# One fused layer, forward and backward: key and query projections in turns, earlier value rows, an earlier output gradient, and x kept in the home of w2

## The chip, the core and the metric

The kernel runs on one core of a Trainium2 chip. The metric is device time in microseconds (us) of one execution; lower is better. PE is the matrix engine, DVE the vector engine, ACT the scalar engine, POOL the general engine, which also issues DMAs, and SP an engine that does nothing but issue DMAs. Each engine works off its own instructions strictly in order; between engines there are only semaphores.

## The reference

One transformer layer on 2048 tokens of width 512, in bf16: an attention sublayer and a feed-forward sublayer, each behind a layer norm and inside a residual sum. The kernel returns the layer's output and the gradients with respect to x, wqkv, wo, w1, b1, w2 and b2, for a given output gradient.

```python
def _A_ref(x, wqkv, wo):                 # 32 heads of 16
    W, dil = 8, 2
    q, k, v = ...                        # x @ wqkv, split by heads
    idx = pos[:, None] - (jnp.arange(W) * dil)[None, :]
    ...                                  # keys and values at idx, masked where idx < 0
    logits = jnp.einsum("bhsd,bhswd->bhsw", q, kg) * scale
    attn = _softmax(logits, axis=-1)
    o = jnp.einsum("bhsw,bhswd->bhsd", attn, vg)
    return (...) @ wo
def _B_ref(x, w1, b1, w2, b2):
    return _gelu(x @ w1 + b1) @ w2 + b2
h  = x + _A_ref(_layernorm(x), A_wqkv, A_wo)
h2 = h + _B_ref(_layernorm(h), B_w1, B_b1, B_w2, B_b2)
# and jax.vjp of this with respect to all operands but B_x
```

So every token attends to eight tokens: itself and those 2, 4, ... 14 places back.

## The kernel before, in words

The 2048 tokens are four chunks of 512 (`NC` = 4, `CH` = 512). There are three stages.

**Stage 1, attention forward** (lines 346 to 516). For each chunk `c` these helpers run:

- `p1_ln` (L352): SP loads the rows of x, DVE forms statistics (L196, L197), POOL the inverse deviation `rstd` (L201), DVE the normalised rows `ln1` (L205); POOL stores them in DRAM (`ln_d`, L181), PE transposes them (L189) and ACT copies the result to `ln1T` (L190). There are three buffers for x of chunks 0 to 2, one for chunk 3, and one buffer for `ln1`.
- `p1_qk` (L374): `p1_proj` (L366) makes four groups of the key (`kt`), then four of the query (`qt`). A group is four matmuls `ps_qkv` (L370) and one ACT copy (L372). Three small columns of the key go on to the next chunk (DVE copy L383).
- `p1_dots` (L398): for each of the four groups DVE multiplies query and shifted keys (`pr`, L259), and PE sums the products into the logits `ps_L` (L263). There are two product buffers.
- `p1_sm1`, `p1_sm2` (L403, L425): softmax, as a chain over engines: ACT `asb`, DVE `m` (L409), ACT `m1h`, DVE `m` (L413), ACT `m2h`, DVE `m` (L417), PE L419, ACT `e` (L422), PE `ps_sum` (L430), DVE reciprocal (L434), PE `ps_r` (L437), ACT `rb` (L439), DVE `attn` (L440).
- `p1_v` (L388): the value projection, PE transposes to token order (`ptm`, L237), ACT copies `tmst` (L240), SP stores rows `v_d` (L242). `p1_tm` (L394) does the same for key and query, `k_d` and `q_d`.
- `p1_o(c, 0)` and `p1_o(c, 1)` (L443): POOL gathers rows of `v_d` into `R` (L251; two buffers), DVE multiplies them with the attention weights (`prb`, L289), PE sums (`ps_band`, L294), ACT copies `ost` (L453), POOL stores `o_d` (four DMAs, L456), PE transposes (`ptu`, L306), ACT copies `oT` (L307).
- `p1_d` (L459): output projection `ps_wo` with x added by an identity matmul (L466, L467), ACT copies `h` (L468), then the second layer norm into `ln2T`.

`p1_round(c)` (L489) mixes these over neighbouring chunks. Inside a round the program calls `p1_ln(c+2)`, `p1_dots(c+1)`, `p1_d(c-1)`, `p1_qk(c+2)`, `p1_sm1(c+1)`, `p1_o(c,0)`, `p1_v(c+1)`, `p1_sm2(c+1)`, `p1_o(c,1)`, `p1_tm(c+1)`. The framework's scheduler settles the final order of each engine's instructions in stages 1 and 2; the order of calls is its priority. It also inserts the waits, among them those of a buffer for its last readers.

**Stage 2, feed-forward, forward and backward** (lines 518 to 754). `p2_h(c)` (L558) makes the hidden layer in four blocks of up to four column tiles: PE `ps_h` (L571), ACT L572 and L573, then a chain of DVE operations and one ACT sigmoid (L576 to L584), which leaves the activation `gt` and its derivative `dt`; SP transposes `gt` by DMA (`tst`, L555), POOL stores it (`gT_d`, L556). `p2_rest(c)` (L590) makes the layer's output with w2 (`ps_f`, L602), then the gradient of the hidden layer: PE `ps_gg` (L615), from the transposed output gradient `goT` and the transposed weights `w2T`, and DVE L617, which multiplies it into `dt`; then the gradient of the layer norm's output, `ps_gl` (L626), with the transposed `w1T`. SP issues the transposing DMAs in this order: `woT`, three parts of `w2T` (L703), four parts of `w1T` (L705), stores of the hidden layer, and then `goT` of chunk 0 (L594).

**Stage 3, attention backward and weight gradients** (from line 760) has an order written out by hand and is not touched.

**Weights.** w1 and w2 (in three parts each, homes `w10`, `w18`, `w112` and `w20`, `w28`, `w212` of the pool `wff`) are loaded by POOL near the start (L485, L487). At the very start SP issues, in this order: the biases b1 and b2 (L149, L151), x of chunk 0, four small stores of zero rows (L347), three parts of wqkv (L358), x of chunks 1 to 3 (L178).

Of the kernel before, what the change touches and what calls it, by code (L numbers as in the profile page):

```python
# [10 lines left out]
P = 128  # L11
BF16 = mybir.dt.bfloat16
# [8 lines left out]
PAD = 16  # L21
# [15 lines left out]
def kernel(  # L37
# [108 lines left out]
    rstd1 = const.tile([P, NT], F32, name="rstd1")  # L146
    rstd2 = const.tile([P, NT], F32, name="rstd2")
    b1b = const.tile([FT, P], BF16, name="b1b")
    SY.dma_start(out=b1b[:], in_=B_b1.rearrange("(f p) -> f p", p=P))  # L149
    b2row = const.tile([1, D], BF16, name="b2row")  # L150
    SY.dma_start(out=b2row[:], in_=B_b2.rearrange("(a n) -> a n", a=1))  # L151
    b1c = const.tile([P, FT], F32, name="b1c")
    gb1p = const.tile([P, FT, NC], F32, name="gb1p")

# [181 lines left out]
                return t_[:, f - a, :]  # L336

    w1 = wparts(wff, "w1", W3, False)
    w2 = wparts(wff, "w2", W3, True)
    late = LP("late")  # L340
    early = LP("early", "right")

    wqkv = early.tile([P, DC, 3 * D], BF16, name="wqkv")
    wo = late.tile([P, DC, D], BF16, name="wo")

    for (d_t, r) in ((v_d[0], 0), (k_d[0], 0), (q_d[NC - 1], CH), (go_d[NC - 1], CH)):
        SY.dma_start(out=d_t[r:r + RPAD, :], in_=zrow[:])  # L347

    st_ = [dict() for _ in range(NC)]
    h_all = []  # L350

    def p1_ln(c):  # L352
        xt = (early if c < NC - 1 else late).tile([P, TPC, D], BF16, name="xt", tag="xt", bufs=NC - 1 if c < NC - 1 else 1)
        load_rows(xt, xf, c)
        if c == 0:
            for i in range(3):
                o = (1, 0, 2)[i] * D
                SY.dma_start(out=wqkv[:, :, o:o + D], in_=A_wqkv[:, o:o + D].rearrange("(a p) j -> p a j", p=P))  # L358
        ln1 = early.tile([P, TPC, D], BF16, name="ln1", tag="ln1", bufs=1)
        layernorm(early, xt, rstd1, c, ln1)  # L360
        store_rows(ln1_d, c, ln1)
        ln1T = early.tile([P, DC, CH], BF16, name="ln1T", tag="ln1T", bufs=2)
        to_fm(ln1, ln1T)
        st_[c].update(xt=xt, ln1T=ln1T)

    def p1_proj(c, sel, dst, off):  # L366
        for g in range(4):
            ps = X("ps_qkv")
            for dc in range(DC):
                T.matmul(ps[:], lhsT=wqkv[:, dc, sel * D + g * P:sel * D + (g + 1) * P],  # L370
                         rhs=st_[c]["ln1T"][:, dc, :], start=(dc == 0), stop=(dc == DC - 1))
            A.copy(out=dst[:, g, off:off + CH], in_=ps[:])  # L372

    def p1_qk(c):  # L374
        qt = early.tile([P, 4, CH], BF16, name="qt", tag="qt", bufs=2)
        kt = early.tile([P, 4, PAD + CH], BF16, name="kt", tag="kt", bufs=2)
        if c == 0:
            V.memset(kt[:, :, 0:PAD], 0.0)
            zz = early.tile([P, 4, PAD], BF16, name="zz", tag="zz")
            V.memset(zz[:], 0.0)  # L380
            G.dma_start(out=vf_d[:, :, 0:PAD], in_=zz[:])
        else:
            V.tensor_copy(out=kt[:, :, 0:PAD], in_=st_[c - 1]["kt"][:, :, CH:CH + PAD])  # L383
        p1_proj(c, 1, kt, PAD)
        p1_proj(c, 0, qt, 0)
        st_[c].update(qt=qt, kt=kt)

    def p1_v(c):  # L388
# [9 lines left out]
    def p1_dots(c):  # L398
        d = st_[c]
        d["L"] = [X("ps_L") for _ in range(2)]  # L400
        dots(late, d["qt"], d["kt"], d["L"], c == 0)
# [73 lines left out]
    p1_ln(0)  # L475
    p1_qk(0)
    p1_dots(0)
    G.dma_start(out=wo[:], in_=A_wo.rearrange("(a p) j -> p a j", p=P))
    p1_ln(1)
    p1_v(0)  # L480
# [2 lines left out]
    p1_sm2(0)  # L483
    for a_, b_, t_ in w1:
        G.dma_start(out=t_[:], in_=B_w1[:, a_ * P:b_ * P].rearrange("(a p) f -> p a f", p=P))  # L485
    for a_, b_, t_ in w2:
        G.dma_start(out=t_[:], in_=B_w2[a_ * P:b_ * P, :].rearrange("(a p) d -> p a d", p=P))  # L487
    p1_tm(0)
    def p1_round(c):  # L489
        if c + 2 < NC:  # L490
            p1_ln(c + 2)
        if c + 1 < NC:
            p1_dots(c + 1)
        if c > 0:
            p1_d(c - 1)
        if c + 2 < NC:
            p1_qk(c + 2)
        if c + 1 < NC:
            p1_sm1(c + 1)
        p1_o(c, 0)  # L500
        if c == NC - 1:
            return
        p1_v(c + 1)
        p1_sm2(c + 1)
        p1_o(c, 1)
        p1_tm(c + 1)
        if c == 0:
            pb = TT("pb1")
            T.transpose(pb[:, 0:FT], b1b[:], ident[0:FT, 0:FT])
            V.tensor_copy(out=b1c[:], in_=pb[:, 0:FT])  # L510
# [79 lines left out]
    def p2_rest(c):  # L590
        d = ps2[c]
        gts, dts = d["g"], d["d"]
        goT = ft("goT")
        SY.dma_start_transpose(out=goT[:], in_=gof[c * CH:(c + 1) * CH, :])  # L594
        gout = ft("gout")
        load_rows(gout, gof, c)
        ln2 = ft("ln2r")
        load_rows(ln2, ln2_d, c)
        for j in range(TPC):
            ps = psT.tile([P, 512], F32, name="ps_f2", tag="t")  # L600
            for f in range(FT):
                T.matmul(ps[:], lhsT=gts[f // 4][:, f % 4, j * P:(j + 1) * P], rhs=wrow(w2, f), start=(f == 0), stop=False)  # L602
            T.matmul(ps[:], lhsT=ones_row[:], rhs=b2row[:], start=False, stop=False)
            T.matmul(ps[:], lhsT=ident[:], rhs=h_all[c][:, j, :], start=False, stop=True)
            h2s = ft("h2s")
            A.copy(out=h2s[:], in_=ps[:])
            A.dma_start(out=h2f[c * CH + j * P:c * CH + (j + 1) * P, :], in_=h2s[:])
            yield
        for bi, (f0, f1) in enumerate(FB):
            for fp in range(f0, f1, 2):  # L610
                for i in range(2):
                    f = fp + i
                    ps = Y("ps_gg")
                    for dc in range(DC):
                        T.matmul(ps[:], lhsT=wcol(w2T, dc, f), rhs=goT[:, dc, :], start=(dc == 0), stop=(dc == DC - 1))  # L615
                    dsl = dts[bi][:, f - f0, :]
                    V.tensor_tensor_reduce(out=dsl, in0=ps[:], in1=dsl, scale=1.0, scalar=0.0,  # L617
                                           op0=ALU.mult, op1=ALU.add, accum_out=gb1p[:, f, c:c + 1])
                yield
            tok_store(dts[bi], f0, f1, ghT_d, c)  # L620
        gh = htile(f"gh{c}")
        gh_all[c] = gh
        for j in range(TPC):
            ps = psT.tile([P, 512], F32, name="ps_gl2", tag="t")
            for f in range(FT):
                T.matmul(ps[:], lhsT=dts[f // 4][:, f % 4, j * P:(j + 1) * P], rhs=wrow(w1T, f),  # L626
                         start=(f == 0), stop=(f == FT - 1))
            t = c * TPC + j
            ln_bwd(ffp["B"], ps[:], ln2[:, j, :], rstd2[:, t:t + 1], gout[:, j, :], gh[:, j, :])
            yield  # L630
# [70 lines left out]
    w1T = wparts(wfb, "w1T", W4, True)  # L701
    for a_, b_, t_ in w2T:
        SY.dma_start_transpose(out=t_[:], in_=B_w2[a_ * P:b_ * P, :])  # L703
    for a_, b_, t_ in w1T:
        SY.dma_start_transpose(out=t_[:], in_=B_w1[:, a_ * P:b_ * P])  # L705
    run(hn)
# [496 lines left out]
```

## Time and profile before

| what | value |
|---|---|
| median of 6 executions | 691.83 us (685.3 to 698.63) |
| the profiled execution | 693.65 us, of which its span is 691.6 us |
| busy in the span | PE 614.7 us (89%), DVE 513.6 (74%), ACT 368.4 (53%), POOL 148.6 (21%) |
| mean granted clock of PE | 0.973 |
| PE busy, 0 to 177 us (stage 1 and the first hidden blocks) | 140.4 us |
| DVE busy, 0 to 177 us | 148.9 us |
| PE and DVE busy, 204 to 260 us (stage 2) | 54.7 and 43.7 us of 56 |

The span runs from the first to the last instruction of the profiled execution; the rest of its time (693.65 - 691.6 = 2.05 us) lies around it. Times in the traces count from the start of the span. A line of a timeline gives the start, the length, the engine, the source line, the operation with output and inputs, how many instructions are merged (x8), and in brackets how long the engine had been idle before and what released it. Busy times of the stretches in the last three rows are sums over a table of stretches of the span.

### The profile page before, as it was taken

What the parts mean: (1) busy time and instruction counts of PE and PEld (TensorE: products, weight loads), DVE (VectorE), ACT (ScalarE), POOL (GpSimd) and SP (SyncE); (2) the same over time, 40 slices, a digit from 0 to 9 for tenths busy, and PEclk for the clock granted to TensorE, in tenths of its full rate; (3) what the DMA queues carried; (4) which work ended last, traced back from release to release, by engine and by line L of the source; (5) the groups of instructions that cost most, each with busy time, mean ns of one, the idle gap of its engine ahead of it and who ended that gap; (6) DMA issues with size and microseconds to landing.
All of it is one profiled execution on the core that took longest, in us unless ns stands there. A gap on an engine that the chain in (4) does not pass through costs nothing. (4 is left out here: it accounts for less than half of the span.)

```text
span 691.6 us, 10209 instructions
## 1 busy us (share of the span) xinstructions
PE 614.7 (89%) x3886; PEld 290.7 (42%) x3948; DVE 513.6 (74%) x758; ACT 368.4 (53%) x576; POOL 148.6 (21%) x183
## 2 busy tenths in 40 slices
PE   2898888787959999999998878989979999988997
PEld 1343443433424434444344333434447667533443
DVE  7879889589758869869843988877987798396400
ACT  1587786688645456456313461673376347463311
POOL 5222534323001101110101122220222124030100
PEclk9999999888979999999999999999999999999999
DMA  8782838636998996998999689756698589979241
GB/s 277 261 285 73 272 120 280 185 136 141 239 232 197 196 228 147 197 237 209 244 236 248 214 303 389 250 201 258 213 405 308 195 291 326 334 280 309 72 152 46
DMA packets 147806, 158.87 MB, mean 230 GB/s; under 512 B 94461, under 2 KB 132398, under 8 KB 141102
## 3 DMA queue, kind: packets, MB, share of 16 engines
q1 hardware_dynamic: 120078, 69.58, 40.2%
q0 software_dynamic: 15376, 77.63, 32.4%
q10 hardware_dynamic: 12304, 11.01, 5.0%
q8 instruction: 31, 0.51, 0.3%
q14 instruction: 17, 0.14, 0.1%
HBM read 87.63 MB, written 48.03 MB: 196 GB/s over the span
## 5 line engine op out<-in xcount | busy, mean ns | idle before, releaser
L985 DVE TENSOR_TENSOR prb<-R,cf 128x2048 bf16<-128x2048 bf16 x96 | 111.4, 1219 | 12.5 <-PE ps_band L993 7.1
L615 PE MATMUL ps_gg<-goT,w2T 128*128 128x512 bf16 x221 | 55.8, 391 | 7.4 <-DMA goT<-in_grad_out_dram 7.1
L617 DVE CUSTOM_DVE_ANT_0 dt<-ps_gg,dt 128x512 bf16<-128x512 f32 x56 | 38.0, 687 | 29.5 <-PE ps_gg L615 29.5
L571 PE MATMUL ps_h<-ln2T,w 128*128 128x512 bf16 x219 | 56.7, 391 | 1.9 <-ACT xa L573 1.2
L869 PE MATMUL ps_gw<-gout_r,gwm 128*128 128x512 bf16 x215 | 53.9, 393 | 3.6 <-DMA gwm<-gT_d 2.8
L211 ACT ACTIVATE gyr<-ps_gl,rstd 128x512 bf16<-128x512 f32 x32 | 22.0, 687 | 63.7 <-PE ps_gl L1049 32.0
L626 PE MATMUL ps_gl<-w1T,dt 128*128 128x512 bf16 x218 | 52.2, 379 | 3.9 <-ACT tmst L240 2.6
L877 PE MATMUL ps_gw<-gwm,ln_r 128*128 128x256 bf16 x448 | 53.8, 275 | 0.9 <-ACT gwst L796 0.7
L572 ACT ACTIVATE xb<-ps_h,b1c 128x512 bf16<-128x512 f32 x56 | 38.9, 701 | 29.1 <-PE ps_h L571 24.1
L602 PE MATMUL ps_f<-w,gt 128*128 128x512 bf16 x218 | 51.0, 379 | 0.9 <-DVE gt L579 0.6
L370 PE MATMUL ps_qkv<-ln1T,wqkv 128*128 128x512 bf16 x185 | 47.5, 394 | 1.6 <-ACT ln1T L190 0.6
L877 PEld LDWEIGHTS <-ln_r 128*128 128x128 bf16 x448 | 42.8, 98 | 13.2 <-issue 6.9
L639 DVE TENSOR_TENSOR pr<-got,vw 128x4096 bf16<-128x4096 bf16 x16 | 36.3, 2289 | 15.1 <-DMA vw<-vf_d 9.8
L897 PE MATMUL ps_gwq<-gqh,ln_r 128*128 128x512 bf16 x188 | 42.2, 379 | 1.5 <-ACT gwst L796 1.3
L573 ACT ACTIVATE xa<-ps_h,b1c 128x512 bf16<-128x512 f32 x56 | 38.8, 703 | 6.5 <-DVE dt L584 6.5
L289 DVE TENSOR_TENSOR prb<-R,cf 128x2048 bf16<-128x2048 bf16 x32 | 37.5, 1207 | 5.7 <-DMA R<-v_d,rowi 5.7
L993 PE MATMUL ps_band<-prb,S 128*32 128x512 bf16 x384 | 31.2, 391 | 10.9 <-DVE prb L985 5.4
L556 POOL DMA_DIRECT2D gT_d<-tst x16 | 12.0, 750 | 129.2 <-DMA tst<-gt 126.6
L240 ACT COPY tmst<-ptm 128x1024 bf16<-128x1024 bf16 x32 | 31.4, 1020 | 14.1 <-PE ptm L237 5.9
L995 ACT ACTIVATE gks<-ps_band 128x512 bf16<-128x512 f32 x32 | 19.0, 598 | 36.7 <-PE ps_band L993 31.5
L615 PEld LDWEIGHTS <-w2T 128*128 128x128 bf16 x224 | 22.3, 99 | 36.9 <-issue 13.3
L259 DVE TENSOR_TENSOR pr<-qt,kt 128x4096 bf16<-128x4096 bf16 x16 | 35.9, 2280 | 1.5 <-PE ps_band L294 0.9
(183 smaller groups left out, 1124.7 us busy)
## 6 DMA issues: line engine op xcount, KB each, us to landing
gwm<-ghT_d SPq DMA_DIRECT2D x7, 1024.0 KB
gT_d<-tst POOLq DMA_DIRECT2D x12, 512.0 KB
ghT_d<-tst POOLq DMA_DIRECT2D x12, 512.0 KB
gwm<-gT_d SPq DMA_DIRECT2D x6, 1024.0 KB
out_dram<-gwst ACTq DMA_DIRECT2D x22, 256.0 KB
ln_d<-ln POOLq DMA_DIRECT2D x8, 512.0 KB
vw<-vf_d SPq DMA_DIRECT2D x4, 528.0 KB
xt<-in_A_x_dram SPq DMA_DIRECT2D x4, 512.0 KB
```

Of the source, the lines that this page charges most:

```text
L370: T.matmul(ps[:], lhsT=wqkv[:, dc, sel * D + g * P:sel * D + (g + 1) * P], rhs=st_[c]["ln1T"][:, dc, :], start=(dc == 0), stop=(dc == DC - 1))
L571: T.matmul(ps[:], lhsT=wcol(w1, dc, f), rhs=ln2T[c][:, dc, :], start=(dc == 0), stop=(dc == DC - 1))
L572: A.activation(out=xb[:, f - f0, :], in_=ps[:], func=ACT.Identity, bias=b1c[:, f:f + 1])
L573: A.activation(out=x2[:, f - f0, :], in_=ps[:], func=ACT.Square, bias=b1c[:, f:f + 1])
L602: T.matmul(ps[:], lhsT=gts[f // 4][:, f % 4, j * P:(j + 1) * P], rhs=wrow(w2, f), start=(f == 0), stop=False)
L615: T.matmul(ps[:], lhsT=wcol(w2T, dc, f), rhs=goT[:, dc, :], start=(dc == 0), stop=(dc == DC - 1))
L617: V.tensor_tensor_reduce(out=dsl, in0=ps[:], in1=dsl, scale=1.0, scalar=0.0, op0=ALU.mult, op1=ALU.add, accum_out=gb1p[:, f, c:c + 1])
L626: T.matmul(ps[:], lhsT=dts[f // 4][:, f % 4, j * P:(j + 1) * P], rhs=wrow(w1T, f), start=(f == 0), stop=(f == FT - 1))
L869: yield from mm_pair("ps_gw2", lambda ps, o, u, i, t, k: T.matmul(ps[:], lhsT=g_[:, o, i * HN + t, :], rhs=gout_r[i][:, t, :], **k), MM, w ...
L877: yield from mm_pair("ps_gw1", lambda ps, o, u, i, t, k: T.matmul(ps[:, 256 * u:256 * u + 256].rearrange("p (a f) -> p a f", a=2), lhsT=ln ...
L897: yield from mm_pair("ps_gwq", lambda ps, o, u, i, t, k: T.matmul(ps[:], lhsT=ln1_r[i][:, t, (2 * d2 + o) * P:(2 * d2 + o + 1) * P], rhs=h ...
L985: V.tensor_tensor(out=pr[:, 4 * hf:4 * hf + 4].rearrange("p j (d h) -> p j d h", h=H), in0=R[:, o:o + 4, :].rearrange("p j (d h) -> p j d ...
```

## The change

1. The biases and the zero rows are issued by SP behind x of chunk 0, wqkv and the first products, not ahead of them.
2. x of chunk 0 and of chunk 1 live in the homes of the first and second part of w2 (`w20`, `w28`). The three loads of w2 are issued on POOL behind `p1_tm(2)` in round 1, and each of these two waits until PE has read the x in its home (L467 of `p1_d(0)` and `p1_d(1)`). The room gives `ln1` a second buffer.
3. `p1_qk` makes key and query groups in turns: k0, q0, k1, q1, and so on.
4. In round 2 the values of chunk 3 (`p1_v(3)`) are called ahead of that chunk's softmax and of `p1_o(2, 0)`.
5. `goT` of chunk 0 is loaded between `w2T` and `w1T`.

```diff
-    SY.dma_start(out=b1b[:], in_=B_b1.rearrange("(f p) -> f p", p=P))
-    SY.dma_start(out=b2row[:], in_=B_b2.rearrange("(a n) -> a n", a=1))
...
-    w2 = wparts(wff, "w2", W3, True)
+    w2 = []
...
-    for (d_t, r) in ((v_d[0], 0), (k_d[0], 0), (q_d[NC - 1], CH), (go_d[NC - 1], CH)):
-        SY.dma_start(out=d_t[r:r + RPAD, :], in_=zrow[:])
...
     def p1_ln(c):
-        xt = (early if c < NC - 1 else late).tile([P, TPC, D], BF16, name="xt", tag="xt", bufs=NC - 1 if c < NC - 1 else 1)
+        xp, xg = ((wff, "w20"), (wff, "w28"), (early, "xt"), (late, "xt"))[c]
+        xt = xp.tile([P, TPC, D], BF16, name="xt", tag=xg, bufs=1)
...
-        ln1 = early.tile([P, TPC, D], BF16, name="ln1", tag="ln1", bufs=1)
+        ln1 = early.tile([P, TPC, D], BF16, name="ln1", tag="ln1", bufs=2)
...
-    def p1_proj(c, sel, dst, off):
-        for g in range(4):
+    def p1_proj(c, sel, dst, off, gs=range(4)):
+        for g in gs:
...
-        p1_proj(c, 1, kt, PAD)
-        p1_proj(c, 0, qt, 0)
+        for g in range(4):
+            p1_proj(c, 1, kt, PAD, [g])
+            p1_proj(c, 0, qt, 0, [g])
...
     p1_dots(0)
+    for (d_t, r) in ((v_d[0], 0), (k_d[0], 0), (q_d[NC - 1], CH), (go_d[NC - 1], CH)):
+        SY.dma_start(out=d_t[r:r + RPAD, :], in_=zrow[:])
+    SY.dma_start(out=b1b[:], in_=B_b1.rearrange("(f p) -> f p", p=P))
+    SY.dma_start(out=b2row[:], in_=B_b2.rearrange("(a n) -> a n", a=1))
...
-    for a_, b_, t_ in w2:
-        G.dma_start(out=t_[:], in_=B_w2[a_ * P:b_ * P, :].rearrange("(a p) d -> p a d", p=P))
     p1_tm(0)
     def p1_round(c):
...
+        if c == NC - 2:
+            p1_v(c + 1)
...
-        p1_v(c + 1)
+        if c < NC - 2:
+            p1_v(c + 1)
         p1_sm2(c + 1)
         p1_o(c, 1)
         p1_tm(c + 1)
+        if c == 1:
+            w2.extend(wparts(wff, "w2", W3, True))
+            for a_, b_, t_ in w2:
+                G.dma_start(out=t_[:], in_=B_w2[a_ * P:b_ * P, :].rearrange("(a p) d -> p a d", p=P))
...
-        goT = ft("goT")
-        SY.dma_start_transpose(out=goT[:], in_=gof[c * CH:(c + 1) * CH, :])
+        goT = goT0.pop() if c == 0 else ft("goT")
+        if c > 0:
+            SY.dma_start_transpose(out=goT[:], in_=gof[c * CH:(c + 1) * CH, :])
...
+    goT0 = [ft("goT")]
+    SY.dma_start_transpose(out=goT0[0][:], in_=gof[0:CH, :])
     for a_, b_, t_ in w1T:
         SY.dma_start_transpose(out=t_[:], in_=B_w1[:, a_ * P:b_ * P])
```

The scheduler takes these up as follows in the built kernel. On PE, DVE and ACT of stage 1 and of the first third of stage 2 instructions change places; from the second chunk's `ps_f` on PE's order is that of before. On SP the order changes only in the points 1 and 5. On POOL the load of the third part of w2 stays near the start, the first stands behind the two gathers of chunk 1, the second behind the two gathers of chunk 2.

## The prediction

> **What bounds the kernel now.** I read the slices of the page first, for where PE is not full.
>
> ```profile
> PE   2898888787959999999998878989979999988997
> ...
> DVE  7879889589758869869843988877987798396400
> ...
> PEclk9999999888979999999999999999999999999999
> ```
>
> A slice is 17.3 us. From the 13th slice on PE stands at 8 or 9; before, neither PE nor DVE is full, and the whole change lies there. So a gain there moves the rest forward as a block: the table of PE's waits has nothing above 0.3 us from 205 to 320 us. Next, the waits of DVE and of PE in the first 206 us, longest first.
>
> ```profile
> DVE prb L289 <- DMA R<-v_d,rowi: 5.7, 1, 5.7
> DVE nm L203 <- POOL rstd L201: 5.1, 5, 1.2
> ...
> DVE ln L205 <- DMA ln_d<-ln: 2.9, 1, 2.9
> ...
> DVE kt L383 <- PE ps_qkv L370: 2.4, 1, 2.4
> DVE attn L440 <- ACT rb L439: 1.8, 1, 1.8
> ```
>
> ```profile
> PE pt L189 <- DVE ln L205: 15.9, 4, 11.4
> PE ps_gg L615 <- DMA goT<-in_grad_out_dram: 7.1, 1, 7.1
> ```
>
> The numbers are the sum, how often, and the longest. 11.4 of PE's 15.9 us are the start. Four entries are what the change aims at: the value rows R (5.7), the store of ln1 that holds its one buffer (2.9), the keys (2.4), goT (7.1). Up to 177 us DVE is the tighter engine (busy 148.9 us, PE 140.4), so for that part I count DVE's idle time; behind 177 us I count PE's. The last place in detail, PE's timeline and then SP's:
>
> ```profile
> 204.36 3.57 PE L615 MATMUL ps_gg<-goT,w2T 128*128 128x512 bf16 x8 [7.07 <-DMA goT<-in_grad_out_dram]
> 207.73 1.06 PE L571 MATMUL ps_h<-ln2T,w 128*128 128x512 bf16 x2
> 208.58 1.80 PE L615 MATMUL ps_gg<-goT,w2T 128*128 128x512 bf16 x4
> ...
> 213.03 1.89 PE L615 MATMUL ps_gg<-goT,w2T 128*128 128x512 bf16 x8
> ```
>
> ```profile
> 171.26 11.99 SPq L703 DMA_TRANSPOSE w2T<-in_B_w_dram  x3
> 183.29 10.15 SPq L705 DMA_TRANSPOSE w1T<-in_B_w_dram  x4
> 193.55 4.98 SPq L555 DMA_TRANSPOSE tst<-gt  x2
> 198.64 1.94 SPq L594 DMA_TRANSPOSE goT<-in_grad_out_dram  x1
> ```
>
> goT is issued behind 10.15 us of w1T and 4.98 us of stores, lands 5.7 us later, and PE has stood since 197.3. Then eight matmuls take 3.57 us where later eight take 1.89.
>
> **The change part by part.** All against the profiled execution (span 691.6, its own time 693.65 us; it is 1.82 us slower than the median, so I subtract the sum from the median).
>
> *Start.* SP issues x of chunk 0 at 1.53 us, behind the biases; it will be at 0.74, where b1 is now: 0.8 us for the chain x, statistics, ln1, keys. The six small issues (0.46 + 0.23 + 0.41 + three of 0.32 = 2.1 us) now stand ahead of x of chunks 1 to 3 on SP; x of chunk 1 goes out at about 0.74 + 0.41 + 1.50 (wqkv) + 2.1 = 4.8 us, against 5.09 now, so nothing is late. Ends 0 and 0.8.
>
> *Keys and queries in turns, second ln1 buffer.* In chunk 0 DVE's first product is at 22.07 us. ACT's first copy ends at 18.21, the second at 19.06, and in the new order that second is the first query, so the first product can start at 18.3 (with the 0.8 from the start), 3.8 us earlier. DVE now has 2.86 us of waiting for ln_d and, at chunk 1, 2.40 + 0.29 us for keys and query: 5.55 us that can go. ACT's copies of the groups follow each other by 0.87 us, so a pair takes 1.7; DVE takes 2.22 for a product, so it is fed. What comes in its place: 0.85 us for the first pair (DVE's statistics end at 17.4); 0.9 us at the key columns L383, which wait for the fourth key, now seventh of eight groups; and 1.9 us in chunk 1's order: today a product stands between the reciprocal (ends 45.52) and attn, in the new order attn follows at once, and rb, behind two tmst copies on ACT, ended at 47.35. Behind that waiting attn stand two products and the transposes of chunk 0's band. 0.8 + 5.55 - 0.85 - 0.9 - 1.9 = 2.7 by idle time; following the chain instruction by instruction to the first band (54.58 us now) gives 2.0. I take **2.3** with the start; ends -1 (rb later by three more copies and ln1T) and 6.3 (all of it).
>
> *Order around the second layer norm.* In chunk 0 DVE waits 0.94 us at 84.8 for rstd; the new order has a band product there. Later PE is as tight as DVE there (reciprocal waits 1.36 us for ps_sum), so I take **0.4**; ends 0 and 0.9.
>
> *Values of chunk 3.* Now the tmst copies run at 122.53 and 124.69 on ACT, between ost copies; SP stores at 123.57 and 125.7; POOL's gather goes out at 129.20 (the profile names the last band product, 128.96; the second store is as late), and DVE waits 5.68 us for the rows until 137.44. The new ACT order has both tmst copies right behind the ln2T copies, which end at 120.77: they end at about 121.9 and 123.1, the second 2.6 us earlier. ost moves behind them and ends at 124.3, its four stores take 2.15 on POOL, so the gather goes out at about 126.6. rb is no longer behind an oT copy either, which brings the last band product forward by 2. Thus **2.4**, of 5.68 that could go at most; lower end 0, if w2's second part, now queued on POOL 16 us ahead of this gather, slows the rows (DMA share 0.39 in that stretch).
>
> *w2 later.* Its two large parts leave POOL behind the gathers of chunks 1 and 2 and wait for L467. Behind each stands rstd of the second layer norm, for which DVE waits in order. But rstd needs the same matmuls, then ACT's copy and DVE's statistics, so the added wait ends first, and the issue costs 0.8 us inside those (POOL idle 6.04 and 4.83 us before rstd). Issued near 80 and 110 us, needed at 176.95 by L602: hidden by some 55 us; were that cover gone, each us late would cost one. No gain or loss.
>
> *goT.* Issued behind w2T, so from about 183.3, it lands near 189 by its own 5.7 us; PE needs it at 195 to 197. PE's 7.07 us go. Then the half clock: from 204.36 to 210.22 PE does 14 matmuls in 5.86 us; at the 0.215 us of the eight from 213.03 they take 3.0. The table of stretches shows the granted clock 0.52 in 199.90 to 210.50 and 1.00 before and after; other dips (0.87 in 135.4 to 149 and in 169.5 to 183) also hold a PE stop of 2.92 and 2.98 us. So another 2.8 us could go: 9.9. But DVE, idle 8.8 us there for L617, cannot gain more than that, and its own chain waits for sigmoids (1.37 us each). I take **8.5**, between ends 5 (three sigmoid waits and the clock dip stay: 9.9 - 2.8 - 2.1) and 9.9. Next late: w1T, pushed back by goT's 2 to 3 us, lands around 200 in today's times and is needed by L626 at 216.9 - 9.9 = 207: hidden by 7 us.
>
> The Trainium skill (TensorE: Matmul & The Clock Gate, "Part 1: The HAM clock gate") says that PE falls to half rate after an idle window of about 3.4 us and needs a busy window to return. This case's dip after 7.07 us of idle agrees. By that rule the goT term is 8.5 only because of DVE; were the dip independent of the stop, it would be 7.1 and the sum 12.2.
>
> **Sum:** 2.3 + 0.4 + 2.4 + 8.5 = 13.6 us. 691.83 - 13.6 = **678.2 us** (the profiled execution: 680.0). With all lower ends (-1, 0, 0, 5) 687.8; with all upper ends (6.3, 0.9, 5.7, 9.9) 669.0.
>
> **Rivals.**
> 1. *Stage 1 gives nothing in the end.* Its stops are links between engines, and a DVE freed earlier may just wait for the next gather; the rows of chunk 2 are needed by DVE at 113.78, 6.5 us after their second gather left POOL. Then only goT remains: 691.83 - 8.5 = 683.3. Against: gathers hang on values, which move forward as well.
> 2. *goT is early but little follows.* PE's stop becomes several short ones at L617 and L626: from 206 to 230 us DVE is 22 of 24 us busy. Goes to the lower end 5 with stage 1 halved (2.5): 684.3; with stage 1 at nothing 686.8.
> 3. *Slower: the softmax chain stretches.* ACT works in order, and with turns four query copies (0.59 us each) can come between each chunk's asb, m1h, m2h, e and rb; in chunk 0 m1h already waited over 2 us behind ln1T and tmst copies. At 2.4 us for chunks 1 to 3 it eats 7.1. It decides from (8.5 + 2.4 + 0.4 + 2.3) / 3 = 4.5 us per chunk; at 6 us the time is 691.83 + 18 - 13.6 = 696.2. Against: from 54.6 to 78 us DVE had only 0.3 us of idle, with softmax beside other products.
> 4. *More than I take:* rows of chunk 3 on time and all of chunk 0's stop gone: 3.3 + 3.0 more, 672.
>
> **How the numbers follow.** Forecast 0.66, rival 1 0.13, rival 2 0.10, rival 3 0.05, rival 4 0.06. The forecast's own range is 674 to 683. The 80% range takes in rivals 1, 2 and 4: 671 to 687. About 1% (6.9 us) is what a measurement of this kernel can tell from no change. Faster by over 1% (under 684.9) are the forecast, rival 4, and most of 1 and half of 2, less a share for the scatter of runs: 0.79. Within 1%: 0.16. Slower: 0.05.
>
> **What the profile will show.** Right: the first product L259 near 18.3 us; no wait of ln for ln_d; chunk 3's first band rows gathered 2 to 3 us sooner relative to the band before; no wait of ps_gg for goT, and full clock where 0.52 stood; ps_f (L602) starting near 172 instead of 176.95. Wrong: a new DVE wait at attn for rb of over 2 us, a wait of L626 for w1T or of L602 for w2, a half clock that stays at ps_gg, or waits of PE for DVE that add up to more than 2 us up to 230 us.

## The result and the profile after

The changed kernel takes 684.51 us (median of 21 executions, 678.87 to 691.81), beside 693.1 us for the kernel before on the same chips (42 executions). The ratio is 0.9886, 95% interval [0.9863, 0.991]: 1.1% or 7.9 us faster. The profiled execution took 683.0 us, with a span of 681.0 against 691.6.

The slices of the page first.

```profile
PE   3689998878899899999997989899979999988997
...
DVE  6779989779879869869843979887987799296400
...
PEclk9799999988899999999999979999999999999999
```

The hole at the 12th slice (PE 5) is a 9 now: that was goT. But the second slice, 17 to 34 us, is worse than before: PE 6 where 8 stood, DVE 7 where 8 stood, and a clock digit of 7. DVE's waits in the first 206 us say what it is (total, times, longest):

```profile
DVE st L194 <- DMA xt<-in_A_x_dram: 9.9, 3, 6.1
DVE prb L287 <- DMA R<-v_d,rowi: 5.8, 2, 5.1
...
DVE m L406 <- PE pt L187: 2.3, 1, 2.3
DVE attn L437 <- ACT rb L436: 1.7, 1, 1.7
...
DVE st L194 <- ACT h L465: 1.2, 1, 1.2
```

The waits for ln_d (2.9) and for the keys (2.4) are gone, as intended. In their place stands the first line: statistics wait for x three times, 9.9 us, where there was one wait of 3.4. That one, for x of chunk 0, is now 2.45; the other two, 7.5 us, are new. The start in the timelines of SP and DVE:

```profile
4.62 0.70 SPq L477 DMA_DIRECT2D b1b<-in_B_b_dram  x1
5.86 0.23 SPq L478 DMA_DIRECT2D b2row<-in_B_b_dram  x1
8.81 2.37 SPq L176 DMA_DIRECT2D xt<-in_A_x_dram  x3
```

```profile
13.06 1.29 DVE L194 BATCH_NORM_STATS2 st<-xt 128x6 f32<-128x512 bf16 x2 [1.40 <-DMA xt<-in_A_x_dram]
...
22.03 0.69 DVE L194 BATCH_NORM_STATS2 st<-xt 128x6 f32<-128x512 bf16 x1 [6.06 <-DMA xt<-in_A_x_dram]
...
23.30 4.48 DVE L257 TENSOR_TENSOR pr<-qt,kt 128x4096 bf16<-128x4096 bf16 x2
```

x of chunk 1 goes out at 8.81 us (5.09 before; forecast 4.8). DVE stands 6.06 us for x of chunk 2, whose statistics are ahead of the first product in its order, and that product starts at 23.30 (22.07 before; forecast 18.3) although its query had long been there. At the other end, PE at goT's place, and SP:

```profile
192.47 3.62 PE L577 MATMUL ps_h<-ln2T,w 128*128 128x512 bf16 x16
195.92 1.89 PE L622 MATMUL ps_gg<-goT,w2T 128*128 128x512 bf16 x7
...
198.50 1.02 PE L622 MATMUL ps_gg<-goT,w2T 128*128 128x512 bf16 x4 [0.47 <-DVE gb1p L624]
```

```profile
172.21 13.27 SPq L710 DMA_TRANSPOSE w2T<-in_B_w_dram  x3
185.59 2.34 SPq L712 DMA_TRANSPOSE goT<-in_grad_out_dram  x1
187.98 9.85 SPq L714 DMA_TRANSPOSE w1T<-in_B_w_dram  x4
```

No wait for goT, and the first group of matmuls runs at once at full clock: the granted clock in 199.9 to 210.5 us is 1.00 (0.52 before).

Four marks put every kernel of this study side by side, in us of its profiled execution: DVE's first product, chunk 0's first band product on DVE, and on PE the first output matmul `ps_f` of chunk 0 (stage 1 is over) and the first `ps_f` after 205 us (chunk 1; goT's place is passed). Times and ratios are over all executions.

| kernel | first product | first band | ps_f, chunk 0 | ps_f, chunk 1 | median us | ratio to before, 95% interval |
|---|---|---|---|---|---|---|
| before | 22.07 | 54.58 | 177.0 | 237.51 | 693.1 | 1 |
| changed | 23.30 | 58.51 | 177.8 | 229.72 | 684.51 | 0.9886 [0.9863, 0.991] |
| small_front | 17.99 | 50.82 | 173.4 | 225.25 | 677.79 | 0.9788 [0.9739, 0.9837] |
| x_first | 18.27 | 50.52 | 172.0 | 223.66 | 679.03 | 0.9806 [0.9755, 0.9858] |
| bias_behind_x | 17.29 | 50.13 | 169.8 | 221.97 | 677.08 | 0.9794 [0.9756, 0.9832] |
| w1_held | 18.81 | 53.70 | 174.5 | 226.52 | 684.96 | 0.985 [0.9781, 0.992] |
| goT_only | 22.14 | 54.95 | 177.6 | 229.29 | 683.54 | 0.9887 [0.984, 0.9933] |
| stage1_only | 22.23 | 57.39 | 176.7 | 237.57 | 692.2 | 0.9928 [0.9878, 0.9977] |
| small_only | 26.29 | 59.91 | 182.2 | 238.32 | 695.79 | 1.0059 [1.0018, 1.01] |
| sf_no_turns | 20.61 | 52.40 | 174.2 | 225.85 | 682.16 | 0.98 [0.9748, 0.9853] |
| sf_v_back | 19.18 | 52.12 | 173.3 | 224.97 | 681.7 | 0.9791 [0.9748, 0.9834] |
| sf_ln1_one | 18.16 | 50.73 | 172.7 | 224.79 | 682.7 | 0.9813 [0.9765, 0.986] |
| sf_od_sp | 19.05 | 51.95 | 173.0 | 229.77 | 680.69 | 0.9777 [0.9732, 0.9822] |
| sf_both | 18.45 | 51.29 | 183.1 | 234.82 | 689.4 | 0.9983 [0.9946, 1.002] |

The groups ran on different chips with their own runs of the kernel before, so medians of different groups are compared by the ratios. Executions more than 1.5% above the fastest of the same kernel are left out of the ratios but not of the medians; for stage1_only that is 7 of 12, the profiled one among them, which is why its ratio and its median do not fit together.

Read before against changed: -0.8 for stage 1 (177.0 to 177.8), and +7.8 up to chunk 1's ps_f, so 8.6 from goT. Behind that the order of PE is the same in both, and the spans differ by another 2.8 us there (454.1 against 451.3). That part moves by itself: over these kernels it is 449.1 to 459.7 us.

### The profile page after: what moved, and what is told of

It reads as the page before. It is cut to its first block, busy times and chain, and to the rows that moved or that the text cites. A ratio compares the mean times of both kernels' runs of the same rounds, so it can differ in the third digit from the quotient of the medians.

```text
span 681.0 us, 10208 instructions
## 1 busy us (share of the span) xinstructions
PE 610.6 (90%) x3887; PEld 288.3 (42%) x3948; DVE 512.9 (75%) x758; ACT 368.6 (54%) x576; POOL 148.4 (22%) x183
## 5 line engine op out<-in xcount | busy, mean ns | idle before, releaser
L886 PE MATMUL ps_gw<-gwm,ln_r 128*128 128x256 bf16 x448 | 53.5, 275 | 0.7 <-ACT gwst L805 0.7
L622 PE MATMUL ps_gg<-goT,w2T 128*128 128x512 bf16 x220 | 53.3, 378 | 0.9 <-DVE gb1p L624 0.5
L633 PEld LDWEIGHTS <-dt 128*128 128x128 bf16 x224 | 21.0, 97 | 33.2 <-issue 7.0
```

What stands on the lines that cost most here:

```text
L886: yield from mm_pair("ps_gw1", lambda ps, o, u, i, t, k: T.matmul(ps[:, 256 * u:256 * u + 256].rearrange("p (a f) -> p a f", a=2), lhsT=ln ...
```

## The experiments

Theory 1: the six small issues ahead of x pushed x of chunks 1 to 3 back, and this ate what the other parts of stage 1 had gained. Theory 2: the turns of keys and queries stretch the softmax chain, whatever x does. Theory 3: DVE waits for the next gather anyway, so nothing gained in stage 1 can reach stage 2.

### small_front: the six issues back at the front

The order on DVE and PE stays that of the changed kernel.

```diff
+    SY.dma_start(out=b1b[:], in_=B_b1.rearrange("(f p) -> f p", p=P))
+    SY.dma_start(out=b2row[:], in_=B_b2.rearrange("(a n) -> a n", a=1))
...
+    for (d_t, r) in ((v_d[0], 0), (k_d[0], 0), (q_d[NC - 1], CH), (go_d[NC - 1], CH)):
+        SY.dma_start(out=d_t[r:r + RPAD, :], in_=zrow[:])
...
     p1_dots(0)
-    for (d_t, r) in ((v_d[0], 0), (k_d[0], 0), (q_d[NC - 1], CH), (go_d[NC - 1], CH)):
-        SY.dma_start(out=d_t[r:r + RPAD, :], in_=zrow[:])
-    SY.dma_start(out=b1b[:], in_=B_b1.rearrange("(f p) -> f p", p=P))
-    SY.dma_start(out=b2row[:], in_=B_b2.rearrange("(a n) -> a n", a=1))
```

> The changed kernel with the six small issues of SP (biases and zero rows) back where they were, ahead of x and wqkv; everything else of the change stays, and DVE's and PE's order are those of the changed kernel. Theory 1 (the six issues pushed x of chunks 1 to 3 from 5.09 to 8.81 us, into POOL's weight loads, and DVE's 6.06 + 1.40 + 2.45 us of waiting for x is what ate the gain of stage 1): x of chunk 1 goes out near 5.1 us, DVE has no wait for x but the first, the first product starts at 18.5 to 19.5 us instead of 23.30, chunk 0's first band product at 54 to 55.5 instead of 58.51, the first output matmuls of stage 2 at 173 to 175 instead of 177.77, and the time is 3 to 5 us below the changed kernel's, 11 to 13 below the kernel before. Theory 2 (the turns of keys and queries stretch the softmax chain, whatever x does): the first product comes forward, but DVE then waits 2 us or more for the logits and for rb, the first band product stays at 57 or later, stage 2 starts at 177 to 178, and the time is within 1 us of the changed kernel's. Theory 3 (DVE waits for the next gather anyway): the first band comes forward by 3 or more, but the start of stage 2 by less than 1.

In its timelines of SP and DVE:

```profile
5.05 3.16 SPq L178 DMA_DIRECT2D xt<-in_A_x_dram  x3
```

```profile
17.99 4.49 DVE L259 TENSOR_TENSOR pr<-qt,kt 128x4096 bf16<-128x4096 bf16 x2 [1.21 <-ACT qt L373]
...
43.71 0.69 DVE L442 TENSOR_TENSOR attn<-e,rb 128x1024 bf16<-128x1024 bf16 x1 [1.74 <-ACT rb L441]
...
50.82 1.18 DVE L289 TENSOR_TENSOR prb<-R,cf 128x2048 bf16<-128x2048 bf16 x1
```

Only six tiny DMAs stand elsewhere, and the first product comes 5.3 us sooner than in the changed kernel, the first band 7.7, stage 2 4.4. The ratio 0.9788 stands against 0.9886, so 1% or some 6.8 us (0.0098 x 693) better; at chunk 1's ps_f it is 4.5 us ahead. Theory 1 holds, and the late x cost more than it had put down (first band at 54 to 55.5, 3 to 5 us of time). Theory 2 falls as a cause of the loss: attn waits for rb by the same 1.74 us in both kernels. Theory 3 is right in part: of 7.7 us at the band 7.5 are left at the first rows of chunk 2 (116.29 to 108.84), 5.6 at those of chunk 3 (137.50 to 131.95) and 4.4 at stage 2.

### x_first and bias_behind_x: what holds x back

x_first puts the loads of x of chunks 1 to 3 (`load_x`, the first lines of `p1_ln`) directly behind wqkv and all six small issues behind them; bias_behind_x keeps the four zero rows ahead of x and puts only the two biases behind it. Both kernels differ from the changed kernel in a few places of stage 1's order on DVE and PE too. The edit of bias_behind_x:

```diff
...
     p1_ln(0)
-    p1_qk(0)
-    p1_dots(0)
     for (d_t, r) in ((v_d[0], 0), (k_d[0], 0), (q_d[NC - 1], CH), (go_d[NC - 1], CH)):
         SY.dma_start(out=d_t[r:r + RPAD, :], in_=zrow[:])
+    xts += [load_x(c) for c in range(1, NC)]
     SY.dma_start(out=b1b[:], in_=B_b1.rearrange("(f p) -> f p", p=P))
     SY.dma_start(out=b2row[:], in_=B_b2.rearrange("(a n) -> a n", a=1))
+    p1_qk(0)
+    p1_dots(0)
```

> The changed kernel with x of chunks 1 to 3 issued right behind wqkv and the six small issues behind them. It keeps the 0.8 us of the earlier x of chunk 0; the scheduler's order on DVE and PE differs a little from the changed kernel's in stage 1. Theory 1: x of chunk 1 goes out near 3 us, no wait of DVE for x but the first, the first product at 18 to 18.6 us, chunk 0's first band at 53.5 to 55, stage 2's first output matmuls at 172.5 to 175, the time 4 to 6 us below the changed kernel's (12 to 14 below the kernel before). Theory 2: a first product at 18 to 19 but a first band at 57 or later, and no gain on the changed kernel. Theory 3: an early first band, but stage 2 still at 177 to 178.

> The changed kernel with only the two bias loads moved, from ahead of x of chunks 1 to 3 to behind them; the four zero rows stay ahead. SP's issues of the two took 0.70 and 0.23 us. It asks why x of chunk 1 went out as late as 8.81 us. If a DMA of this queue waits for the landing of the one eight places before it: x of chunk 1 becomes the ninth and waits for x of chunk 0 alone, so it goes out at 4.4 to 5.6 us, three to four us sooner; the next two wait for the first and second part of wqkv and go out near 6.5 and 8.8; the first product starts at 18 to 19.2 us instead of 23.30, stage 2 at 172 to 175, and the time is 4 to 8 us below the changed kernel's. If it is plain queueing behind the small issues: x of chunk 1 goes out at 7.6 to 8.1, 0.9 sooner, and the first product is at 22 or later.

x_first: x of chunk 1 at 2.88 us, first product at 18.27, stage 2 at 172.0, the ratio 0.9806: as theory 1 has it, with the first band again sooner than its 53.5 to 55. The telling run is bias_behind_x: two issues of together 0.93 us (0.70 + 0.23) are moved, and x of chunk 1 goes out 4.06 us sooner, at 4.75. That isn't plain queueing. SP's own waits, of the changed kernel and then of bias_behind_x, name what it waited for:

```profile
SPq L176 <- DMA wqkv<-in_A_wqkv_dram: 3.7, 2, 2.7
...
SPq L478 <- DMA wqkv<-in_A_wqkv_dram: 0.5, 1, 0.5
```

```profile
SPq L176 <- DMA wqkv<-in_A_wqkv_dram: 3.5, 2, 2.7
SPq L482 <- DMA wqkv<-in_A_wqkv_dram: 1.1, 1, 1.1
```

And one of x_first's, where b2row is issued at L483:

```profile
SPq L483 <- DMA xt<-in_A_x_dram: 1.2, 1, 1.2
```

The loads of x and of the biases have nothing to do with wqkv. Count the places on SP: in the changed kernel x of chunk 0 is the first DMA, wqkv the second to fourth, the zero rows the fifth to eighth, the biases ninth and tenth, x of chunk 1 the eleventh. b2row (10th) waits for a part of wqkv, x of chunks 1 and 2 (11th, 12th) for others: each for the DMA about eight places ahead of it. In bias_behind_x x of chunk 1 is ninth, behind x of chunk 0 that has landed, and x of chunks 2 and 3 (10th, 11th) and the first bias (12th) wait. In x_first x of chunk 1 is fifth and b2row thirteenth, and b2row waits for x. In the kernel before and in small_front x of chunk 0 is third and x of chunk 1 eleventh, so it has only that to wait for, and the table of SP's waits has no wqkv in it. Eight places fits SP's waits at the start of all fourteen kernels; that a DMA waits for the landing of the one eight places ahead is inferred from these waits, not seen as such.

### w1_held: late issue or shared engines

```diff
-        st_[c].update(xt=xt, ln1T=ln1T)
+        st_[c].update(xt=xt, ln1T=ln1T, ln1=ln1)
...
     for a_, b_, t_ in w1:
+        G.tensor_copy(out=t_[:, 0, 0:1], in_=st_[1]["ln1"][:, 3, 0:1])
         G.dma_start(out=t_[:], in_=B_w1[:, a_ * P:b_ * P].rearrange("(a p) f -> p a f", p=P))
```

(POOL's load of the third part of w2, 0.25 MB, takes the place of the first of w1.)

> The changed kernel with POOL's three loads of w1 (1.8 MB) held until the normalised rows of chunk 1 are written, by a one-column copy on POOL into each home; SP's order at the start stays that of the changed kernel, with x of chunk 1 at 8.8 us, and DVE's order too. It asks what made x of chunk 2 so late. If the shared DMA engines did it: x of chunk 2 lands some 5 us sooner, DVE's wait of 6.06 us shrinks under 1.5, the wait of 1.40 stays, the first product starts at 18 to 20 us, and the time is 2 to 4 us below the changed kernel's. If the late issue alone did it: the wait stays at 5 or more, and the time is within 1 us of the changed kernel's. Under theory 2 the time is that of the changed kernel in both cases.

DVE's waits for x and for rb in the first 60 us:

```profile
DVE st L194 <- DMA xt<-in_A_x_dram: 5.5, 3, 2.6
DVE attn L437 <- ACT rb L436: 3.7, 1, 3.7
```

With w1 out of the way the longest wait falls from 6.06 to 2.60 us, and the first product starts at 18.81, though x is still issued at 8.07 (8.81 in the changed kernel). So the late issue alone would cost little; that x of chunk 2 came at 22.03 us and not at 17.54 was in the main the collision with POOL's 1.8 MB of w1. The Trainium skill (DMA: Bandwidth & Descriptors, "Issuing engines are not separate DMA queues") says that DMAs issued from several engines run on the same DMA engines and interleave; this run agrees: one load was there 4.5 us sooner when another engine's loads were held back, and of that only some 0.74 us are the earlier issue on its queue. My bound of 1.5 us for the wait was too low, and attn now waits 3.67 us for rb (ACT had stood 1.8 us for a `tmst` buffer that a `k_d` store held), so the first band is only at 53.70. Stage 2 comes 3.3 us sooner than in the changed kernel; the ratio 0.985 [0.9781, 0.992] cannot tell it from the changed kernel's.

### small_only: the move of the six issues, alone, on the kernel before

The edit is the first part of the change, which the diff further up shows: the biases and the zero rows leave their places (L149, L151, L347) and stand behind `p1_dots(0)`.

> The kernel before with only the first part of the change: the six small issues behind x of chunk 0 and wqkv; DVE's order is that of the kernel before. If this move alone is what cost stage 1 its gain: x of chunk 1 goes out near 8.8 us instead of 5.09, DVE waits 4 to 8 us for x of chunks 1 and 2 ahead of its first product, the first product starts at 23.5 to 25.5 instead of 22.07 (2.86 us of the waiting lay behind the store of ln1 before), chunk 0's first band at 56 to 58 instead of 54.58, and the time is 1 to 3 us above the kernel before. If it costs only together with the other parts: x late too, but the first band within 0.8 us of 54.58.

```profile
22.38 0.69 DVE L194 BATCH_NORM_STATS2 st<-xt 128x6 f32<-128x512 bf16 x1 [6.98 <-DMA xt<-in_A_x_dram]
...
26.29 6.68 DVE L257 TENSOR_TENSOR pr<-qt,kt 128x4096 bf16<-128x4096 bf16 x3
```

Slower by 0.6%, 4.1 us (0.0059 x 690.8), with interval [0.2, 1.0]%; the first band comes 5.3 us later and stage 2 5.2. That is more than I expected (1 to 3 us). I had thought that 2.86 us of the waiting would lie where DVE had waited for ln_d; but the work that DVE did ahead of that wait, statistics of chunk 2 and ln1 of chunk 1, now stands behind the late x, so the first product comes 3.9 us after x, where before it came 0.97 us after the end of the wait for ln_d.

Most of the 5.2 us do not get past goT, though. PE's wait for it, 7.1 us in the kernel before, is smaller here:

```profile
PE ps_gg L615 <- DMA goT<-in_grad_out_dram: 3.7, 1, 3.7
```

At chunk 1's ps_f only 0.8 us are left (238.32 against 237.51). So the 4.1 us of the ratio are not explained by the marks: the rest lies behind them, in the part that moves by itself. It also says that a late stage 1 costs little as long as goT is late too, so the two gains do not simply add up.

### goT_only and stage1_only: the two halves of the change

goT_only is the kernel before with the fifth part of the change, stage1_only the changed kernel without it (the same lines taken out). The edit of goT_only:

```diff
-        goT = ft("goT")
-        SY.dma_start_transpose(out=goT[:], in_=gof[c * CH:(c + 1) * CH, :])
+        goT = goT0.pop() if c == 0 else ft("goT")
+        if c > 0:
+            SY.dma_start_transpose(out=goT[:], in_=gof[c * CH:(c + 1) * CH, :])
...
+    goT0 = [ft("goT")]
+    SY.dma_start_transpose(out=goT0[0][:], in_=gof[0:CH, :])
     for a_, b_, t_ in w1T:
```

> The kernel before with only the fifth part of the change: goT of chunk 0 between w2T and w1T. If this part carries the whole gain of the change (stage 1 gave -0.8 us): the first output matmuls of stage 2 start at 176.5 to 177.5 as before, the wait of 7.07 us for goT and the half clock at 200 to 210 us are gone, and the time is 8 to 9.5 us below the kernel before, so 0 to 1.5 below the changed kernel. If the start of stage 2 was only fast because of other parts, the gain is 5 us or less, with waits of PE for DVE of more than 2 us in place of the one for goT.

> The changed kernel with goT back at its old place, so the four other parts alone. If the parts add up: stage 1 as in the changed kernel (first product near 23.3, first output matmuls of stage 2 at 177 to 178.5), PE's wait of about 7 us for goT and the half clock behind it are back, and the time is within 2 us of the kernel before. If the other parts bring something behind stage 1: 2 to 4 us below the kernel before.

goT_only reaches the changed kernel's whole gain: 0.9887 against 0.9886. From ps_f of chunk 0 to that of chunk 1 it takes 51.7 us (229.29 - 177.6) where the kernel before takes 60.5: 8.8 us for goT. PE's clock from 199.9 to 210.5 us is 1.00, as in the changed kernel. In stage1_only the stop for goT is back (7.83 us), and the clock is 0.56 from 199.9 to 211 us. stage1_only starts stage 2 at 176.7 and passes ps_f of chunk 1 at 237.57, against 237.51 before. By its ratio it is 5.0 us faster than the kernel before (0.0072 x 690.8, interval 1.6 to 8.4), by its median 1.4 us slower; nothing of a gain is seen at the marks, and its executions spread over 20 us (680.92 to 701.27). So whether the other parts bring something behind stage 1 stays open.

### The parts of stage 1, each taken back on small_front

Three edits, one for each kernel: sf_no_turns, sf_v_back, sf_ln1_one.

```diff
-        for g in range(4):
-            p1_proj(c, 1, kt, PAD, [g])
-            p1_proj(c, 0, qt, 0, [g])
+        p1_proj(c, 1, kt, PAD)
+        p1_proj(c, 0, qt, 0)
```

```diff
-        if c == NC - 2:
-            p1_v(c + 1)
...
-        if c < NC - 2:
-            p1_v(c + 1)
+        p1_v(c + 1)
```

```diff
-        ln1 = early.tile([P, TPC, D], BF16, name="ln1", tag="ln1", bufs=2)
+        ln1 = early.tile([P, TPC, D], BF16, name="ln1", tag="ln1", bufs=1)
```

> The mended kernel (the changed kernel with the six small issues ahead of x and wqkv: first product 17.99 us, chunk 0's first band 50.82, first output matmuls of stage 2 at 173.4, 677.8 us) without the turns: four key groups, then four query groups. If the turns are what brought stage 1 forward: the first query is the fifth copy on ACT, four times 0.87 us later, so the first product starts at 20.5 to 22, chunk 0's first band at 53 to 54.6, the output matmuls of stage 2 at 175 to 176.5, and the time is 2 to 3.5 us above the mended kernel's. If the start and the second ln1 buffer did it and the turns nothing: DVE fills the time with statistics and ln1 of chunk 1, the first band stays within 1 us of 50.82, and the time within 1 us.

> The mended kernel with the values of chunk 3 called at their old place. In the mended kernel DVE still waits 5.45 us for the rows of chunk 3 (until 131.95) and then 1.90 us for h, as ACT stands 4.96 us for a tmst buffer that the key stores hold. If the term of the prediction (2.4 us) is right: the rows come 2 to 3 us later, the output matmuls of stage 2 start at 175 to 176.5 instead of 173.4, and the time is 2 to 3 us above the mended kernel's. If the gain is given back at once to ACT's stop and to h: the rows come later, but stage 2 starts within 0.8 us of 173.4, and the time is within 1 us.

> The mended kernel with one ln1 buffer instead of two, so that the rows of chunk 1 wait for the store of those of chunk 0 (2.86 us of DVE's time in the kernel before). If the second buffer is worth what it hides: a wait of DVE for ln_d of 1 to 3 us comes back, chunk 0's first band is at 52 to 54 instead of 50.82, stage 2 starts at 174.5 to 176, and the time is 1 to 3 us above the mended kernel's. If with the turns DVE has products to do until the store has landed: no wait for ln_d, and all within 0.8 us.

Up to chunk 0's bands small_front's order on DVE is also that of sf_v_back, sf_od_sp and sf_both, and their first products range from 17.99 to 19.18 and their first bands from 50.82 to 52.12. So 1.3 us is what one profiled execution cannot tell there.

Without the turns the first product is at 20.61, later by 1.4 to 2.6 us, the first band at 52.40, and stage 2 at 174.2, 0.8 later: less than the first expectation asked for (53 to 54.6; 175 to 176.5), a little more than the second (within 1 us of 50.82). By time it can't be told (0.98 against 0.9788). With one ln1 buffer nothing is lost at all (50.73; 172.7), and no wait for ln_d comes back: with the turns DVE has products to do until the store has landed. Either part alone removes most of the stop that both were meant for.

With the values of chunk 3 back at their old place DVE waits longer for the rows, and still stage 2 starts at 173.3 us. DVE's waits from 110 to 155 us, in small_front and then in sf_v_back:

```profile
DVE prb L289 <- DMA R<-v_d,rowi: 5.5, 1, 5.5
...
DVE st L196 <- ACT h L470: 1.9, 1, 1.9
DVE attn L442 <- ACT rb L441: 1.5, 1, 1.5
```

```profile
DVE prb L289 <- DMA R<-v_d,rowi: 6.7, 1, 6.7
...
DVE attn L442 <- ACT rb L441: 1.5, 1, 1.5
```

The early values bring the rows 1.3 us nearer (6.71 to 5.45 of waiting) and create a wait of 1.90 for h. ACT's waits in small_front show why:

```profile
ACT tmst L240 <- DMA k_d<-tmst: 5.0, 1, 5.0
```

With the value copies early, the key and query copies of chunk 3 meet stores that have not landed; ACT stands 4.96 us for a buffer, with three copies of h queued behind. sf_v_back has no such wait. The second of the two expectations, gain given back at once, is what happened.

### sf_od_sp and sf_both: an attempt on the rows of chunk 3

The first edit is that of sf_od_sp; sf_both has both.

```diff
-            G.dma_start(out=ap, in_=ost[32 * j:32 * j + 32])
+            (SY if (c, sc) == (NC - 2, 0) else G).dma_start(out=ap, in_=ost[32 * j:32 * j + 32])
```

```diff
             p1_d(c - 1)
+        if c == NC - 1:
+            p1_tm(c)
...
-        p1_tm(c + 1)
+        if c < NC - 2:
+            p1_tm(c + 1)
```

> The mended kernel with the four stores of o_d of chunk 2's first half issued by SP behind the value stores, no longer by POOL ahead of the gather of chunk 3. It asks what keeps the rows of chunk 3 late. If it is POOL's queue: the gather goes out at 119.5 to 120.5 us instead of 122.94, the rows are there 2.5 to 3 us sooner, DVE's wait of 5.45 falls to 2.5 to 3, and stage 2 starts 2 to 3 us sooner. If ACT's stop of 4.96 us for a tmst buffer sets the end (h and the second layer norm come behind it): the rows come sooner, DVE's wait for h grows from 1.90 to 3.5 or more, and stage 2 starts within 1 us of 173.4. If neither, and the transfer itself is slower: the rows come as late as before although the gather went out sooner.

> The mended kernel with the stores of o_d of chunk 2's first half on SP, and the token-order copies and stores of key and query of chunk 3 called behind the output projection of chunk 2, so that they do not stand ahead of h on ACT. If gather and ACT's stop were all that held stage 1 back: the rows of chunk 3 at 129 to 130 us, no wait of ACT for a tmst buffer ahead of h, stage 2 at 169.5 to 171.5 instead of 173.4, and 2 to 4 us less than the mended kernel. If behind 135 us PE and ACT are as tight as DVE: the waits go and others come (gt for xa, as the 3.33 us when only the stores were moved), stage 2 starts at 172.5 to 174.5, and the time is within 1.5 us of the mended kernel's.

sf_od_sp: the gather goes out at 121.77 instead of 122.94, though this execution's first band was 1.1 us later; DVE's wait falls to 3.66 us and the rows are there at 129.66, 2.3 sooner. Then DVE waits 3.33 us for ACT's `xa`, an intermediate of the hidden layer, where it waited 0.35, and stage 2 starts at 173.0, 0.4 sooner. Between the two ps_f marks it then takes 4.9 us longer than small_front (56.8 against 51.9), with a wait of PE of 3.3 us for ACT's copy of the output (`h2s`). The ratio is small_front's (0.9777 against 0.9788). So POOL's queue was part of what kept the rows late (a wait of 3.66 us is left), and behind 135 us DVE waits for ACT; but what I had named as next in line (h) was wrong, it was the hidden layer's xa.

sf_both was to free ACT too, and lost nearly all: 0.9983. One line of DVE's waits from 115 to 185 us tells where:

```profile
DVE xa L586 <- ACT xa L583: 12.4, 1, 12.4
```

The token-order copies of chunk 3, put behind the output projection, now stand on ACT ahead of the first hidden block, and DVE, out of other work, waits 12.39 us for it. Stage 2 starts 9.7 us later than in small_front. Neither of its two expectations allowed for that. That these copies alone make the 12.39 us is argued from ACT's order, not shown by a run.

## Why the prediction was right and wrong

The forecast was 678.2 us, the measured time is 684.5: within the range, but the time of the first rival (only goT remains, 683.3). It got there by another mechanism than the rival named: DVE was not freed early to wait for gathers; it was not freed at all. Two of the signs named for stage 1 failed: the first product at 23.30 instead of 18.3, `ps_f` at 177.8 instead of 172. That the time still lay in the range is luck as far as stage 1 goes: the range was wide enough to hold goT alone.

- **The failed step** is in the part on the start: "x of chunk 1 goes out at about 4.8 us, against 5.09 now, so nothing is late". (The 0.8 us of the earlier x of chunk 0 did come: its statistics start at 4.19 us instead of 5.09.) I added up SP's issue times and let the queue run without waiting. It went out at 8.81, as SP waited for wqkv to land; then x collided with w1. Alone this move makes the kernel before 5.2 us later at stage 2 (small_only; 4.1 us in time, interval 1.2 to 6.9); taken back it makes the changed kernel some 6.8 us faster (small_front). The kernel before had no such wait in its trace, and I did not give the step a lower end below nothing although its queue had been rearranged.
- **Keys and queries in turns, second ln1 buffer, with the start: 2.3.** On the mended start the first product comes at 17.99. The forecast was 18.3 with the 0.8 us of an earlier x of chunk 0, which this kernel does not have, so it came 1.1 us sooner than worked out. The first band is 3.8 us sooner than before (54.58 to 50.82), against 2.0 by the chain I had followed. The term was too small. The wait of attn for rb was forecast at 1.9 and is 1.74. The two parts aren't additive: either alone is enough to within 1.6 us.
- **Order around the second layer norm: 0.4.** From the first band to chunk 2's first rows the changed kernel wins 1.4 us on the kernel before (+3.93 at 58.51, +2.51 at 116.29), small_front 1.2. The wait for rstd is gone as foretold; a wait of 0.72 us for rows came in. Mis-sized by 1 us, which is within what one execution cannot tell.
- **Values of chunk 3: 2.4.** Right at its place: the gather goes out at 128.54 where DVE is 2.5 us later than before, so 3.2 us sooner relative to it, and DVE's rows are there as early as before in spite of the later start. But nothing of it reaches stage 2 (sf_v_back: 173.3 against 173.4). The step missed what was late next: ACT's buffers for the token-order copies, and h behind them.
- **w2 later: nothing.** Right. Its parts leave POOL at 83.37 and 113.26 us, and no output matmul waits for w2.
- **goT: 8.5.** Right: 8.6 in the changed kernel, 8.8 alone. The Trainium skill (TensorE: Matmul & The Clock Gate, "Part 1: The HAM clock gate") lets an idle window of about 3.4 us bring the half rate; by the runs the dip at 200 to 210 us goes together with the stop (clock 1.00 in its place), and a new stop of 3.71 us at the start of the changed kernel is followed by a new dip (0.50 from 26.5 to 33.3 us), which small_front, without that stop, does not have (1.00). But the page's 3.4 us is no least length of a stop here: in the kernel before the clock was also 0.50 from 139 to 141 us, behind a stop of 2.92 us. No wait for w1T came.
- **The sum.** With the one step mended, the marks come near the sum: 12.3 us up to ps_f of chunk 1 (237.51 to 225.25) against 13.6 forecast, and 0.9788 in time, 14.7 us (0.0212 x 694.2, interval 11.3 to 18.1). Stage 1 gave 3.6 of the 5.1 us forecast, goT the rest. That the two lie so near is in part luck: the keys' term was too small, and the values' term came to nothing.

A version better than both kernels is thus small_front, x_first or bias_behind_x: 677 to 679 us. By the marks bias_behind_x is ahead (221.97), by time the three are one. What stays open is why bias_behind_x's 3.3 us over small_front at chunk 1's ps_f do not show in the ratio; its profiled execution (683.71 us, 6.6 above its median) had clock dips in the last stage (0.86 in 440 to 460 us, 1.00 there in small_front), which is the scatter named above and no evidence on the change.

## What to carry to other kernels

Moving small DMAs on a queue moves the places of all behind them: read which earlier transfer each will then wait for, not just the sum of issue times, and give every rearranged queue a lower end below zero. A gain at one place must be followed to the next buffer and the next engine until it passes the last mark of the stage; here 7.7 us became 4.4 within some 120 us, and the early values became nothing. And where one kernel holds several changes, compare marks along the trace as well as the total: 8.6 us of gain at one end hid a loss of 4.4 at the other (stage 2 at 177.8 where 173.4 was to be had).

## What the runs showed that I had not expected

SP, which issues DMAs without using their data, was held by the landing of transfers unrelated to its next one: up to 2.7 us at a time, 4.2 in all (3.7 ahead of x, 0.5 ahead of b2row), fitting a turn of eight. Two DMAs of 3.5 and 1 KB ahead of a load of 0.5 MB so cost it 4.06 us. The same PE order from chunk 1's ps_f to the end took 449.1 to 459.7 us in fourteen profiled executions, more than most effects studied here; only the marks ahead of it could tell the parts of stage 1 apart.
